# Token sums of phi on GpSimd, kv products split over two slots, and a new order for the opening of a fused attention and two-layer-MoE kernel

## The chip, the core and the metric

The kernel runs on one core of a Trainium2 chip, in one launch, on the inputs of the reference. The metric is the device time of that launch in microseconds (us), the median over runs. The core has five engines that run side by side, each with its own instruction stream executed in order: TensorE (PE in the profile, with its weight loads under PEld), VectorE (DVE), ScalarE (ACT), GpSimd (POOL) and SyncE (SP), whose queue starts nearly all DMA transfers here. An instruction that waits holds up everything behind it on its engine.

## The reference

Eight batches, eight heads, 576 tokens, head dimension 64, 32 memory slots. Attention over memories, then two dense layers:

```python
a = np.exp(phi - np.max(phi, axis=2, keepdims=True))        # over tokens
a = a / (np.sum(a, axis=2, keepdims=True) + 1e-09)
k_m = np.einsum('bhsm,bhsd->bhmd', a, k)
v_m = np.einsum('bhsm,bhsd->bhmd', a, v)
scores = scale * np.matmul(q, k_m.transpose(0, 1, 3, 2))
attn = softmax(scores)                                      # over the 32 memories
x = np.matmul(attn, v_m)                                    # -> (4608, 512)
h = x @ w_in;  g = s * np.maximum(h, 0.0)**2 + b;  x = g @ w_out       # 512 -> 2048 -> 512
# second layer: 512 -> 1024, x * softmax(x), layer norm, 1024 -> 512
```

The weights w_in and w_out are 64-bit floats of 8 MB each; they are read as pairs of 32-bit words and turned into 32-bit floats on the chip. q, k, v and phi are 32-bit floats.

## The kernel before

Work goes batch by batch; a batch's 576 tokens are two halves (j = 0, 1) of 288. For each batch the products of exp(phi) with k and v (`kv_mm`, PSUM tile `kp`) are divided by the sum of exp(phi) over the tokens (`kv_out`), giving the small memories `km`. v's memories times w_in (`vw_mm`, tile `wp`) let attention and the first layer's first product become one product (`hp` from `aT` and the folded weights); the activation is squared, and a second product with w_out gives `y`.

From batch 1 on, the code loops: `gemm1(n, j)`, then four `gemm2(n, j, d)`, and between these, `slot(n + 1, i)` with i = 0 to 7 prepares the next batch. Slot 0 held the whole of `kv_mem` (`kv_mm`, `kv_sum`, `kv_out`); slot 1 bounds the memories, slots 2 and 3 cut q and the memories into 16-bit halves, load the next batch and take the maximum of its phi, slots 4 to 6 hold scores.

Everything ahead of that, batch 0 and the preparation of batch 1, runs in an order written out by hand, the string `FIRST`. Each word is a step with its indices, and each engine's stream is the order in which the words issue instructions on it:

- `Lphi.n`, `Lkv.nu`, `Lq.ni`, `Lw.fk`, `Lo.dx` load phi, k and v (in two parts), q (four parts), a piece of w_in (8 pieces of 1 MB) and a piece of w_out (8 pieces of 1 MB), all on SP's queue (L337, L359, L368, L1128, L1142). phi has one buffer, so `Lphi.1` can start only when the readers of batch 0's phi are done; the same holds for k and v.
- `phm`, `pht`, `phd`, `pho` take phi's maximum over tokens (DVE L389, PE, DVE L400 and L404, PE); `phb` subtracts it (DVE L442), `phe` is the exponential (ACT L448).
- `km` are the 72 products per batch of phi with k and v (L478, two hardware passes each, 144 rows in the trace). `ks` is `kv_sum_all`: 72 further products of phi with a column of ones (L494), which add up the tokens in PSUM. `ko` is `kv_out`: the DVE reads the sums (L500), inverts them and scales the products.
- `qm`/`qo` transpose q (PE L547, ACT L559); `mm`, `mv`, `mk` transpose the memories; `s0` are scores (PE L830), `s1` their maximum and difference (DVE L842, L844), `s2` the exponential, `s3` sum and reciprocal, `s6` the division (DVE L863); `at`/`aA` transpose the attention.
- `Ai`, `Ci`, `PiX` decode a piece of w_in (ACT L285; DVE L289 and L290; DVE L1186); `Ao`, `Co`, `PoX` the same for w_out; `Bi`, `Bo` sums for scales (ACT L298). `vm`, `vA`, `vD` make the folded weights. `g.jp` is a quarter of the first layer for half j (PE L913), `gr`, `gs` its activation (ACT); `y.dx` half of an output column block of the second layer (PE L941); `Y` the same for half 1 (L1091).

`KEEP` gives, for some steps, a number of dummy products of a tile of ones that PE runs ahead of the step's own (L167); their result is overwritten. The only way in which the streams meet is by waits on semaphores that follow from tiles and buffers; PSUM tile `h` has three buffers, used in turn.

`kv_sum`, a single product per partition half with a precomputed sum `es` (L483), is used for batches 2 to 7, where the DVE makes `es` (`phi_sum`, inside `gemm1`).

Of the kernel before, what the change touches and what calls it, by code (L numbers as in the profile page):

```python
# [64 lines left out]
def tile_mem_attention__moe_relu2__solu_ln(  # L65
# [393 lines left out]
    def kv_mem(n):
        kv_mm(n)  # L460
        kv_sum(n)
        kv_out(n)

    def kv_cells(n):
        for c in range(CT):
# [1200 lines left out]
```

## Time and profile before

| | us |
|---|---|
| median of 3 runs (1096.86 to 1098.18) | 1097.57 |
| the profiled execution's own time | 1096.71 |
| its span, first to last instruction | 1094.9 |
| PE busy | 1058.2 (97%) |
| DVE busy | 766.3 (70%) |
| ACT busy | 523.8 (48%) |
| POOL busy | 177.5 (16%) |
| mean granted TensorE clock | 0.986 |

The span is 1.81 us under the profiled execution's time, which is 0.86 us under the median. A share of the whole span is a mean over stages: the opening (to about 170 us) is nothing like the loop behind it, so the rows below are read by stage. Idle time matters only on an engine that something later waits for.

### The profile page before, as it was taken

The page shows a single profiled execution, that of the slowest core. Times are in us where ns is not written, and L with a number is a line of the kernel's source. Part 1 is how long each engine was busy: PE and PEld are TensorE (multiplying, and loading weights), DVE is VectorE, ACT ScalarE, POOL GpSimd, SP SyncE. Part 2 cuts the span into 40 slices and gives each one's busy share as a digit, 9 for nine tenths or more (in the row PEclk, how much of TensorE's full clock was granted, in tenths as well). Part 3 has the DMA queues.
Part 4 walks back from the last instruction along what each step waited for, and adds up shares of the span by engine and source line. Part 5 has one row for each costly group of instructions (what it writes and reads, how often), then busy time and mean ns, then how long its engine had stood idle before and what let it go on. Part 6 is the DMA issues. An engine that isn't in the chain of part 4 may idle for free.

```text
span 1094.9 us, 21722 instructions
## 1 busy us (share of the span) xinstructions
PE 1058.2 (97%) x8931; PEld 699.3 (64%) x8931; DVE 766.3 (70%) x1456; ACT 523.8 (48%) x775; POOL 177.5 (16%) x165
## 2 busy tenths in 40 slices
PE   3869999999999999999999999999999999999998
PEld 2657768777777777777777777754444444444443
DVE  5468999977767768768778766467666666666662
ACT  3358875754644644654654555433323333233322
POOL 0000020221030030130120110013222221222221
PEclk9689999999999999999999999999999999999999
DMA  9885154652842932932932342124434434435324
GB/s 274 253 239 181 27 143 111 129 132 75 179 111 70 202 95 68 219 77 75 211 102 49 65 159 91 42 60 106 108 100 101 107 93 109 106 87 116 85 60 106
DMA packets 202595, 129.28 MB, mean 118 GB/s; under 512 B 137472, under 2 KB 182528, under 8 KB 202496
## 3 DMA queue, kind: packets, MB, share of 16 engines
q1 hardware_dynamic: 202352, 127.70, 46.5%
q8 instruction: 70, 1.15, 0.5%
q14 instruction: 29, 0.24, 0.1%
q10 hardware_dynamic: 112, 0.20, 0.1%
q0 software_dynamic: 32, 0.00, 0.0%
HBM read 71.83 MB, written 23.07 MB: 87 GB/s over the span
## 4 chain that ended last, share of the span: by engine, by line
PE 92%; DMA 3%; issue 2%; DVE 1%; ACT 1%; SPq 0%; ACTq 0%
PE y L1091 33%; PE y L1494 17%; PE hp L1412 17%; PE hp L1009 15%; PE hp L913 2%; PE kp L478 2%; PE wp L637 2%; PE sp L786 1%; DMA raw<-in_moe_w_in_dram 1%; DMA kv_s<-in_v_dram 1%; PE wp L595 1%; PE y L941 1%; DMA work<-kv_s 1%; PE sp L830 1%; PE tq L547 1%
## 5 line engine op out<-in xcount | busy, mean ns | idle before, releaser
L1091 PE MATMUL y<-g,w_out 128*128 128x288 f16 x2688 | 337.8, 286 | 0.5 <-issue 0.5
L1091 PEld LDWEIGHTS <-w_out 128*128 128x128 f16 x2880 | 277.6, 97 | 87.0 <-issue 13.4
L1412 PE MATMUL hp<-w_t,xs 128*128 128x512 f16 x864 | 192.0, 379 | 0.0
L1494 PE MATMUL y<-w_t,lt 128*128 128x512 f16 x864 | 191.7, 379 | 0.0
L1009 PE MATMUL hp<-aT,vwt 128*128 128x288 f16 x1344 | 166.9, 286 | 0.0
L1009 PEld LDWEIGHTS <-vwt 128*128 128x128 f16 x1344 | 131.5, 98 | 33.1
L1494 PEld LDWEIGHTS <-lt 128*128 128x128 f16 x864 | 84.6, 98 | 101.7
L1412 PEld LDWEIGHTS <-xs 128*128 128x128 f16 x864 | 84.5, 98 | 101.5
L1456 POOL TENSOR_TENSOR rstd<-ve,nhalf 128x1 f32<-128x1 f32 x36 | 52.6, 1462 | 332.4 <-DVE mv L1454 332.4
L1426 DVE TENSOR_REDUCE hmx<-hp 128x1 f32<-128x1024 f32 x36 | 44.1, 1224 | 84.1 <-PE hp L1412 84.1
L318 ACT ACTIVATE xs<-xt,xsc 128x512 f16<-128x512 f32 x36 | 25.9, 720 | 151.0 <-PE hp L1412 129.5
L1020 ACT ACTIVATE r<-hp 128x576 f32<-128x576 f32 x120 | 77.4, 645 | 26.9 <-PE hp L913 14.7
L1074 DVE TENSOR_TENSOR g<-r_s,g 128x576 f16<-128x576 f32 x112 | 85.6, 764 | 3.9
L1108 ACT ACTIVATE x<-y,bcol,cs 128x288 f32<-128x288 f32 x60 | 35.2, 586 | 106.8 <-PE y L1091 96.2
L1067 ACT ACTIVATE r_s<-r 128x576 f32<-128x576 f32 x112 | 76.6, 684 | 18.5 <-DVE g L1074 13.4
L315 DVE TENSOR_REDUCE xmx<-x 128x1 f32<-128x288 f32 x64 | 28.8, 450 | 53.0 <-ACT x L1108 52.9
L994 DVE CAST g<-r_s 128x576 f16<-128x576 f32 x112 | 52.1, 466 | 18.7 <-ACT r_s L1067 18.6
L1433 ACT ACTIVATE e<-hp,nm,xiv 128x1024 f32<-128x1024 f32 x36 | 43.3, 1203 | 45.6 <-DVE nm L1428 45.6
L1502 ACT ACTIVATE o<-y,io 128x512 f32<-128x512 f32 x36 | 24.8, 689 | 53.3 <-issue 40.8
L1470 DVE TENSOR_TENSOR nat<-so,nat 128x1024 f16<-128x1024 f32 x36 | 43.8, 1216 | 5.4 <-ACT nat L1465 5.4
L1449 DVE BATCH_NORM_STATS2 bs<-so 128x6 f32<-128x512 f32 x72 | 46.3, 685 | 1.2
L1444 DVE SCALAR_TENSOR_TENSOR so<-hp,sm,e 128x1024 f32<-128x1024 f32 x36 | 46.2, 1284 | 1.3
(240 smaller groups left out, 1191.4 us busy)
## 6 DMA issues: line engine op xcount, KB each, us to landing
kv_s<-in_k_dram SPq DMA_DIRECT2D x32, 288.0 KB, 9.1
kv_s<-in_v_dram SPq DMA_DIRECT2D x32, 288.0 KB, 9.6
x_d<-x SPq DMA_DIRECT2D x64, 144.0 KB, 1.9
xt<-x_d SPq DMA_DIRECT2D x36, 256.0 KB, 3.1
q_s<-in_q_dram SPq DMA_DIRECT2D x21, 288.0 KB, 4.6
phi_sb<-in_phi_dram SPq DMA_DIRECT2D x16, 288.0 KB, 4.3
out_dram<-o SPq DMA_DIRECT2D x23, 192.0 KB, 2.5
w_out<-in_moe_w_in_dram SPq DMA_DIRECT2D x4, 1024.0 KB, 11.0
```

Of the source, the lines that this page charges most:

```text
L994: nc.vector.tensor_copy(out=g_of(n, j, 0)[:, 2 * fp:2 * fp + 2, 0:BLK], in_=gt["r2", j, fp])
L1009: nc.tensor.matmul(out=hp[:, u, 0:BLK], lhsT=vt[:, pw, R, f * 128:(f + 1) * 128], rhs=aT[:, CJ * j:CJ * (j + 1), pa, R, :], start=(x == 0) ...
L1020: nc.scalar.activation(out=r, in_=gt.pop(("h", j, fp))[:, :, 0:BLK], func=ACTF.Relu, scale=scale)
L1067: nc.scalar.activation(out=r2, in_=r, func=ACTF.Square)
L1074: (nc.vector if eng == "D" else nc.gpsimd).tensor_tensor(out=g_of(n, j, 1)[:, fs, 0:BLK], in0=gt.pop(("r2", j, fp)), in1=g_of(n, j, 0)[:, ...
L1091: nc.tensor.matmul(out=y[:, 0:w], lhsT=w_out_t[d][:, pw, f, :], rhs=g_of(n, j, pg)[:, f, 0:w], start=(x == 0), stop=(x == len(steps) - 1),)
L1412: nc.tensor.matmul(out=hp[:, a, :], lhsT=xs[:, px, kk, :], rhs=wt[:, pw, kk, a * 512:(a + 1) * 512], start=(kk == 0 and px == 0 and pw == ...
L1426: nc.vector.tensor_reduce(out=mx, in_=hv, op=ALU.max, axis=AX)
L1444: nc.vector.scalar_tensor_tensor(out=so, in0=hv, scalar=sm[:, 0:1], in1=e, op0=ALU.mult, op1=ALU.mult)
L1449: nc.vector.bn_stats(out=bs[:, a, :], in_=so[:, a * 512:(a + 1) * 512])
L1456: nc.gpsimd.tensor_tensor(out=rstd, in0=ve, in1=nhalf, op=ALU.pow)
L1494: nc.tensor.matmul(out=y[:, 0:DM], lhsT=lt[:, pl, f, :], rhs=wt[:, pw, f, :], start=(x == 0), stop=(x == len(steps) - 1),)
```

## The change

In batches 0 and 1 the 72 products with ones are gone; five GpSimd additions (`phi_sum_pool`, step `ke`) add the nine token groups of exp(phi) down to `es`, and `ks` is now `kv_sum`, one product per partition half with ones. In later batches `kv_mm` is cut into token groups 0 to 4 in slot 0 and 5 to 8 in slot 1, and `kv_sum` and `kv_out` (with its load of the next phi) move to slot 1. The string `FIRST` and the numbers in `KEEP` are new: 35 dummies before, 109 after.

```diff
 FIRST = """
-Lw.01 Lw.00 Lphi.0 Ai.01 Ci.01 PiX.01 phm.0 Ai.00 Ci.00 Lq.02 qm.02 PiX.00 Lw.10 pht.0 phd.0 pho.0 Lkv.00 Ai.10 Lkv.01
+Lphi.0 phm.0 pht.0 phd.0 pho.0 Lw.10 Ai.10 Ci.10 PiX.10 phb.01 phb.00 Lkv.00 Lkv.01 phe.00 phe.01 ke.0 km.0 Lw.00
...
 KEEP = {
-    "pht.0": 4, "km.0": 8, "vap.0": 3, "qm.03": 1, "qm.00": 2, "qm.02": 10, "s0.00": 2, "pht.1": 4, "at.1": 1,
+    "qm.02": 4, "pht.0": 7, "pho.0": 6, "km.0": 16, "qm.00": 1, "mm.0": 8, "qm.01": 24, "qm.03": 1, "s0.01": 21,
+    "vap.0": 3, "at.1": 5, "at.0": 13,
 }
...
-    def kv_sum_all(n):
-        for out_, ph, ps, i, c, at in kv_cells(n):
-            nc.tensor.matmul(out=out_[:, 2 * D:2 * D + 1], lhsT=ph, rhs=ones[ps, :], **at)
+    def phi_sum_pool(n):
+        ph = phi_t[n]
+        t = e_p.tile([128, HG, 2, M], FP32, tag="pa", name="t", bufs=1)
+        es = e_p.tile([128, HG, M], FP32, tag="es", name="es", bufs=1)
+        for out_, x, y in (
+            (t, ph[:, :, 0:2], ph[:, :, 2:4]), (t, t, ph[:, :, 4:6]), (t, t, ph[:, :, 6:8]),
+            (es, t[:, :, 0], t[:, :, 1]), (es, es, ph[:, :, 8]),
+        ):
+            nc.gpsimd.tensor_tensor(out=out_, in0=x, in1=y, op=ALU.add)
+        es_t[n] = es
...
         if i == 0:
-            kv_mem(n)
+            kv_mm(n, range(0, 5))
...
         elif i == 1:
+            kv_mm(n, range(5, CT))
+            kv_sum(n)
+            kv_out(n)
...
-        "km": kv_mm, "ks": kv_sum_all, "ko": kv_out, "vb": vw_bound, "vs": vw_scale,
+        "km": kv_mm, "ke": phi_sum_pool, "ks": kv_sum, "ko": kv_out, "vb": vw_bound, "vs": vw_scale,
```

Three places show how the streams move. The first is SP's queue from its first transfer to the first load of batch 1's k and v; raw_g, raw and w_out are where pieces of w_in land. Before:

```order
L1128 DMA raw_g<-in_moe_w_in_dram 128x2x1024 x2
L337 DMA phi_sb<-in_phi_dram 64x4x288 x2
L368 DMA q_s<-in_q_dram 96x2x384
L1128 DMA raw<-in_moe_w_in_dram 128x2x1024
L359 DMA kv_s<-in_k_dram 64x2x576 x2
L359 DMA kv_s<-in_v_dram 64x2x576 x2
L359 DMA kv_s<-in_k_dram 64x2x576 x2
L359 DMA kv_s<-in_v_dram 64x2x576 x2
L1128 DMA raw<-in_moe_w_in_dram 128x2x1024
L368 DMA q_s<-in_q_dram 96x2x384 x2
L368 DMA wt_s<-in_q_dram 96x2x384
L337 DMA phi_sb<-in_phi_dram 64x4x288 x2
```

The same stretch of SP's queue after:

```order
L338 DMA phi_sb<-in_phi_dram 64x4x288 x2
L1135 DMA raw<-in_moe_w_in_dram 128x2x1024
L360 DMA kv_s<-in_k_dram 64x2x576 x2
L360 DMA kv_s<-in_v_dram 64x2x576 x2
L360 DMA kv_s<-in_k_dram 64x2x576 x2
L360 DMA kv_s<-in_v_dram 64x2x576 x2
L1135 DMA raw_g<-in_moe_w_in_dram 128x2x1024 x2
L369 DMA q_s<-in_q_dram 96x2x384
L338 DMA phi_sb<-in_phi_dram 64x4x288 x2
L369 DMA q_s<-in_q_dram 96x2x384 x2
L369 DMA wt_s<-in_q_dram 96x2x384
L1135 DMA raw<-in_moe_w_in_dram 128x2x1024
```

phi, then k and v, now stand ahead of all but one piece of w_in, three parts of q stand behind batch 1's phi, and k and v come behind 1.6 MB instead of 4.0 MB.

The second place is PE around batch 1's products (`km.1`, `ks.1`). Before:

```order
L830 MATMUL sp<-kmT,qt_s 96x2x32 x8
L478 MATMUL kp<-kv_s,phi_sb 32x128 x72
L494 MATMUL kp<-ones,phi_sb 32x1 x72
L913 MATMUL hp<-aT_118,vw_522 128x288 x4
L595 MATMUL wp<-w_in_t,first 32x512 x8
```

PE there after:

```order
L599 MATMUL wp<-w_in_t,first 32x512 x8
L468 MATMUL kp<-kv_s,phi_sb 32x128 x72
L480 MATMUL kp<-ones,es 128x1 x2
L917 MATMUL hp<-aT_118,vw_573 128x288 x4
L599 MATMUL wp<-w_in_t,first 32x512 x8
```

The 72 products with ones became two; the scores ahead of the products (`s0.02`, tile `sp`, L830) moved to an earlier place, and folded weights (`vm.02`) stand there instead.

The third place is the DVE's stream from phi's maximum to the division by the sums (`phm.0` to `ko.0`). Before:

```order
L389 TENSOR_REDUCE pm<-phi_sb 128x128
L289 TENSOR_SCALAR w_in_t<-w_in_t 128x2x512
L290 SCALAR_TENSOR_TENSOR w_in_t<-raw_g,w_in_t 128x2x512
L1186 SCALAR_TENSOR_TENSOR w_in_t<-raw_g,w_in_t 128x2x512
L400 TENSOR_REDUCE first<-tx 128x2
L404 TENSOR_TENSOR first<-ident,first 128x256
L442 TENSOR_TENSOR phi_sb<-phi_sb,tx 128x576
L289 TENSOR_SCALAR w_in_t<-w_in_t 128x2x512
L290 SCALAR_TENSOR_TENSOR w_in_t<-raw,w_in_t 128x2x512
L442 TENSOR_TENSOR phi_sb<-phi_sb,tx 128x576
L1186 SCALAR_TENSOR_TENSOR w_in_t<-raw,w_in_t 128x2x512
L500 TENSOR_SCALAR rs<-kp 128x2
```

The DVE there after:

```order
L390 TENSOR_REDUCE pm<-phi_sb 128x128
L401 TENSOR_REDUCE first<-tx 128x2
L405 TENSOR_TENSOR first<-ident,first 128x256
L290 TENSOR_SCALAR w_in_t<-w_in_t 128x2x512
L291 SCALAR_TENSOR_TENSOR w_in_t<-raw,w_in_t 128x2x512
L1193 SCALAR_TENSOR_TENSOR w_in_t<-raw,w_in_t 128x2x512
L443 TENSOR_TENSOR phi_sb<-phi_sb,tx 128x576
L443 TENSOR_TENSOR phi_sb<-phi_sb,tx 128x576
L290 TENSOR_SCALAR w_in_t<-w_in_t 128x2x512
L291 SCALAR_TENSOR_TENSOR w_in_t<-raw_g,w_in_t 128x2x512
L504 TENSOR_SCALAR rs<-kp 128x2
```

phi's maximum is now the DVE's first work, and one and two thirds pieces of w_in are decoded ahead of `ko.0` where before three were (the first of them ahead of the rows shown).

## Rows read from the trace of the kernel before

**Rows 1.** Who waited for whom, 0 to 80 us: total, times, longest
```profile
DVE rs L500 <- PE kp L494: 20.6, 2, 11.1
PE kp L494 <- issue: 11.8, 3, 6.3
```

**Rows 2.** Waits of SP's DMA queue, 0 to 100 us
```profile
SPq L337 <- PE kp L494: 19.7, 2, 13.0
```

**Rows 3.** PE in order of time: start, length, ..., [idle before <- releaser]
```profile
12.74 2.19 PE L547 MATMUL tq<-ident,q_s 96*64 96x96 f32 x24 [9.16 <-DMA q_s<-in_q_dram]
...
18.63 1.89 PE L167 MATMUL kp<-first 128*128 128x256 f16 x8
...
25.94 3.72 PE L478 MATMUL kp<-kv_s,phi_sb 64*32 64x128 f32 x131 [0.57 <-DMA kv_s<-in_v_dram]
...
32.94 1.27 PE L494 MATMUL kp<-ones,phi_sb 64*32 64x1 f32 x119 [3.08 <-issue]
...
43.62 2.82 PE L830 MATMUL sp<-kmT,qt_s 128*96 128x64 f32 x16
...
56.53 8.03 PE L913 MATMUL hp<-aT,vw 128*128 128x288 f32 x32
64.48 1.09 PE L595 MATMUL wp<-w_in_t,first 64*32 64x512 f32 x16
65.50 1.57 PE L830 MATMUL sp<-kmT,qt_s 128*96 128x64 f32 x16
67.00 2.25 PE L478 MATMUL kp<-kv_s,phi_sb 64*32 64x128 f32 x144
...
79.21 0.26 PE L494 MATMUL kp<-ones,phi_sb 64*32 64x1 f32 x2 [6.33 <-issue]
79.41 4.21 PE L913 MATMUL hp<-aT,vw 128*128 128x288 f32 x8
```

**Rows 4.** Stretches: length, then busy us of each engine, granted clock, DMA
```profile
core 0: us, PE busy (x) PEld busy (x) DVE busy (x) ACT busy (x) POOL busy (x), PEclk, DMA share, GB/s
0.00:56.50 56.50, 34.62 (x505) 25.54 (x505) 29.08 (x49) 20.66 (x31) 0.68 (x6) 0.82 0.91 263
34.20:53.00 18.80, 17.36 (x137) 13.32 (x137) 11.54 (x22) 8.93 (x16) 0.00 (x0) 0.50 0.93 299
56.50:69.00 12.50, 12.50 (x211) 9.61 (x212) 12.36 (x16) 11.65 (x21) 0.00 (x0) 1.00 1.05 295
69.00:79.40 10.40, 1.70 (x163) 1.52 (x143) 1.02 (x2) 1.54 (x3) 0.00 (x0) 0.73 0.62 190
79.40:170.10 90.70, 89.94 (x564) 67.22 (x563) 81.27 (x153) 66.50 (x98) 8.16 (x8) 0.97 0.45 114
```

**Rows 5.** ACT in order of time: the first and the fourth decoded piece of w_in
```profile
6.20 1.12 ACT L285 ACTIVATE w_in_t<-raw_g 128x1024 f32<-128x1024 f32 x1 [4.19 <-DMA raw_g<-in_moe_w_in_dram]
...
28.77 1.14 ACT L285 ACTIVATE w_in_t<-raw 128x1024 f32<-128x1024 f32 x1 [5.50 <-DMA raw<-in_moe_w_in_dram]
```

**Rows 6.** Groups by line and shape, 0 to 170 us: busy, mean ns | idle before
```profile
L389 DVE TENSOR_REDUCE pm<-phi_sb 128x128 f32<-128x1152 f32 x3 | 6.4, 2133 | 2.8 <-DMA phi_sb<-in_phi_dram 2.8
...
L289 DVE TENSOR_SCALAR w_in_t<-w_in_t 128x1024 int32<-128x1024 int32 x8 | 5.5, 687 | 5.7 <-ACT w_in_t L285 5.7
...
L290 DVE SCALAR_TENSOR_TENSOR w_in_t<-w_out,w_in_t 128x1024 int32<-128x1024 int32 x4 | 4.9, 1225 | 0.1
...
L1186 DVE SCALAR_TENSOR_TENSOR w_in_t<-w_out,w_in_t 128x1024 int32<-128x1024 int32 x4 | 4.8, 1218 | 0.0
```

**Rows 7.** GpSimd in order of time: two sizes of addition or product
```profile
152.94 2.61 POOL L442 TENSOR_TENSOR phi_sb<-phi_sb,px 128x1152 f32<-128x1152 f32 x1 [9.24 <-issue]
...
226.82 1.05 POOL L863 TENSOR_TENSOR e<-e,ssm 96x512 f32<-96x512 f32 x1 [11.24 <-DVE ssm L858]
```

**Rows 8.** DVE in order of time: one line beside GpSimd's work, and alone
```profile
153.23 2.87 DVE L806 TENSOR_TENSOR e<-e,smx 96x512 f32<-96x512 f32 x1
...
162.60 0.69 DVE L806 TENSOR_TENSOR e<-e,smx 96x512 f32<-96x512 f32 x1
```

**Rows 9.** PE in order of time in the loop, batch 4's sums
```profile
422.85 0.39 PE L483 MATMUL kp<-ones,es 64*128 64x1 f32 x4
```

**Rows 10.** Waits of PE, 170 us to the end: total, times, longest
```profile
PE y L1091 <- issue: 0.5, 1, 0.5
PE kp L478 <- issue: 0.4, 1, 0.4
```

More of the change, by code (lines that the diff above doesn't have):

```diff
@@ new lines @@
+Lw.01 Ai.00 Ci.00 Lq.01 ks.0 ko.0 Ai.01 PiX.00 qm.01 Lphi.1 mm.0 vb.0 Lq.02 qo.01 mv.0 phm.1 Lq.00 mk.0 Ci.01 qm.02
+qo.02 Lq.03 pht.1 Lw.11 qm.00 qm.03 Lw.20 phd.1 qo.00 qo.03 pho.1 Bi.00 PiX.01 s0.00 phb.10 Ai.11 phb.11 Lw.30 Lw.21
+s0.01 Bi.01 s1.00 s2.00 Ci.11 s3.00 PiX.11 s0.02 phe.11 Lw.31 s6.00 Bi.10 Ai.30 phe.10 Ai.20 s1.01 ke.1 Lkv.10 at.0
+aA.0 s2.01 s1.02 s3.01 Ai.21 vm.00 vad.0 vA.00 vm.01 vA.10 vA.11 s6.01 at.1 aA.1 vD.01 Ci.21 Bi.11 s2.02 vap.0 g.00
+Ci.20 g.03 Ai.31 gr.00 gs.0 s3.02 Lkv.11 g.02 PiX.20 g.01 gr.03 gs.3 Bi.20 Lo.01 Lo.11 Lsb s6.02 gr.02 gr.01 PiX.21
@@ new lines @@
+at.2 aA.2 Ci.30 Ci.31 PiX.30 vm.02 gs.2 vA.21 Lo.00 PiX.31 km.1 ks.1 vA.20 Lq.12 ko.1 gs.1 Ao.01 Bi.21 g.04 Ao.11
+Lo.10 mb.1 vm.03 mad.1 vA.30 va.0 g.05 gr.04 vb.1 vA.31 gs.4 Co.01 PoX.01 Lphi.2 vad.1 gr.05 g.06 map.1 Lq.13 Ao.00
+Co.00 PoX.00 gs.5 Lo.20 g.07 gr.06 Bi.30 ma.1 Bi.31 vap.1 Co.11 Lq.10 g.10 im y.00 va.1 gs.6 Ao.10 Bo.00 Lo.21 Lq.11
+iad PoX.11 gr.07 iap Co.10 ia PoX.10 iv vs.0 gs.7 y.01 vr Bo.01 Bo.11 cb.0 Bo.10 gr.10 g.17 yo.00 gh.0 gr.17 qa.10
+om.0 gh.7 oad.0 qa.12 gq.0 Lo.30 oap.0 oa.0 os.0 g.14 ym.00 xh.01 cc.0 qa.11 g.13 xh.00 qa.13 gq.7 xl.01 gl.0 xh.10
@@ new lines @@
+y.10 g.15 gr.14 gh.4 y.11 yd.00 gq.4 xh.11 qs.1 ms.1 Lo.31 xl.00 mm.1 Ao.20 gl.7 Ao.21 gl.4 xl.10 gr.13 gr.15 gh.3
+Co.20 PoX.20 gh.5 gq.3 Co.21 cb.1 gl.3 qh.10 Ao.30 g.12 yo.01 PoX.21 gq.5 gr.12 g.11 y.20 gl.5 gh.2 gq.2 xl.11 mv.1
+Co.30 Ao.31 mh.1 Bo.20 qh.11 Co.31 gr.11 ml.1 y.21 ym.01 gl.2 Bo.21 vm.13 yd.01 PoX.31 PoX.30 ql.10 gh.1 cb.2 g.16
+Bo.31 Bo.30 yo.02 mT.1 vs.1 qT.10 ql.11 vm.10 gq.1 vh.10 phm.2 y.30 om.1 oad.1 gl.1 qT.11 vh.13 ym.02 yd.02 gr.16
+qh.12 vl.13 ql.12 qh.13 oap.1 gh.6 gq.6 oa.1 os.1 qT.12 gl.6 ql.13 pha.2 y.31 cb.3 xh.21 yo.03 ym.03 vl.10 cc.1 vm.11
@@ L55 @@
+qT.13 vh.11 vl.11 vm.12 Y.10 xh.30 xh.20 s0.10 xh.31 sc.10 xl.30 s0.11 sc.11 xl.31 s1.11 s1.10 vh.12 vl.12 Y.00 Y.11
+s2.10 yo.11 Y.01 s3.10 phbP.2 s0.12 s6.10 Y.30 Y.31 s2.11 s3.11 s6.11 phe.2 ym.11 s4.10 s5.10 s4.11 s5.11 xl.20 yo.10
+Lkv.20 sc.12 yd.11 sT.10 s1.12 s2.12 xl.21 yd.03 s3.12 s6.12 ym.10 s4.12 sT.11 Lkv.21 yd.10 yo.13 ym.13 Y.20 Y.21
+Lq.21 yo.12 yd.13 ym.12 yd.12 Lq.20 s5.12 sT.12 Lq.22
 """
 KEEP = {
-    "pht.0": 4, "km.0": 8, "vap.0": 3, "qm.03": 1, "qm.00": 2, "qm.02": 10, "s0.00": 2, "pht.1": 4, "at.1": 1,
+    "qm.02": 4, "pht.0": 7, "pho.0": 6, "km.0": 16, "qm.00": 1, "mm.0": 8, "qm.01": 24, "qm.03": 1, "s0.01": 21,
+    "vap.0": 3, "at.1": 5, "at.0": 13,
@@ L457, in tile_mem_attention__moe_relu2__solu_ln, with kv_mm @@
     kp_t = {}
[L459 to L465, printed above, removed]
+    def kv_mm(n, cs=range(CT)):
+        if cs[0] == 0:
+            kp_t[n] = ps_h.tile([128, 2, 512], FP32, tag="h", name="kp")
+            keep(kp_t[n][:, 1, 256:512])
+        for c in cs:
             for i in range(HG):
@@ L468, in kv_cells @@
                     ps = slice(PT * a, PT * (a + 1))
-                    yield (
-                        kp_t[n][M * i:M * (i + 1), a], phi_t[n][ps, i, c, :], ps, i, c,
-                        dict(start=(c == 0), stop=(c == CT - 1), tile_position=(PT * a, M * i)),
-                    )
-    def kv_mm(n):
-        kp_t[n] = ps_h.tile([128, 2, 512], FP32, tag="h", name="kp")
-        keep(kp_t[n][:, 1, 256:512])
-        for out_, ph, ps, i, c, at in kv_cells(n):
-            nc.tensor.matmul(out=out_[:, 0:2 * D], lhsT=ph, rhs=kv_s[ps, :, i, c * D:(c + 1) * D], **at)
+                    nc.tensor.matmul(
+                        out=kp_t[n][M * i:M * (i + 1), a, 0:2 * D],
+                        lhsT=phi_t[n][ps, i, c, :],
+                        rhs=kv_s[ps, :, i, c * D:(c + 1) * D],
+                        start=(c == 0),
+                        stop=(c == CT - 1),
+                        tile_position=(PT * a, M * i),
+                    )
     def kv_sum(n):
@@ L490, in kv_sum @@
             )
-    def kv_sum_all(n):
-        for out_, ph, ps, i, c, at in kv_cells(n):
-            nc.tensor.matmul(out=out_[:, 2 * D:2 * D + 1], lhsT=ph, rhs=ones[ps, :], **at)
+    def phi_sum_pool(n):
[8 more added lines that the diff above has]
+        es_t[n] = es
     def kv_out(n):
```

19 lines of the change are left out of this document (removed).

## The prediction

> **What bounds the kernel now.** I read the stretches first, then PE in order of time, then the waits. From 170 us on nothing is to be had: PE waits there only twice, 0.5 and 0.4 us [rows 10]. Between 79.4 and 170.1 PE is busy 89.94 of 90.70 us [rows 4], so the opening's second half is PE-bound as well, with the DVE close behind (81.27 of 90.70). What is left is the time up to 79.4. There PE idles: it waits for q (9.16 us) and for k and v, and three times inside the products with ones, for "issue", 11.8 us in all and 6.33 us the longest [rows 1, 3]. "issue" means that nothing the profile knows held PE; the tiny products come so densely (119 in 1.27 us [rows 3]) that I read it as the instruction stream arriving too slowly, which is an inference. While PE stands there, the DVE stands at the division behind it (20.6 us in two waits [rows 1]), and SP's queue stands at the next phi load, whose buffer those products read (19.7 us [rows 2]). In 69.0 to 79.4 all engines are nearly idle at once [rows 4]. And PE is slow: in 34.2 to 53 the granted clock is 0.50, the 1.2 GHz level, after PE's 3.08 us stand [rows 3, 4]; the scores at 43.62 take 2.82 us where the same 16 take 1.57 at 65.50. The column says 1.00 for the first 30 us, yet 24 transposes take 2.19 us there as they do at the low level, so PE probably started low as well.
>
> **The change, part by part.**
>
> *Products with ones, batch 1.* PE leaves the kv products at about 69.1 (67.00 plus 144 rows, 2.25 with overlap) and starts the next quarter at 79.41: 10.3 us. In their place come two products in four rows, 0.39 us [rows 9]. Worth 9.9 us on PE, with no cover: everything is idle. The next quarter then also runs at the full level: 8 rows took 4.21 us, while 32 took 8.03 at 56.53, so 8 cost 2.0 [rows 3]: 2.1 us more. These 12 us follow from the removed line alone.
>
> *GpSimd's sums.* Not in the trace; nearest are 2.61 us for 1152 elements and 1.05 us for 512 [rows 7], 2.3 and 2.05 ns an element. Three additions of 256 and two of 128 are 1024 elements: about 2.2 to 2.4 us a batch, up to 5.3 if each costs as much as the 512-element row. Their cover is long: in batch 0 phi's exponential is done near 15 us while k and v land near 17 (below); in batch 1 `ke.1` stands ahead of four quarters of g, 8 us of PE. So they hold up no product. But they can hold up the DVE. Its difference L806 took 2.87 us at 153.23, when GpSimd worked on phi (152.94 to 155.55), and 0.69 at 162.60 [rows 7, 8]. That is 2.2 us lost beside one addition of 2.61. I charge 2 us for both batches; the ends are 0 and 5.
>
> The Trainium skill (SBUF — State Buffer, Who interferes with whom) says that a DVE instruction with two SBUF inputs contends with a GpSimd instruction that reads SBUF, and that the later one waits for the other's end. L806 fits that. By that rule each of the ten additions may stop one such DVE instruction for its own length, so the DVE could lose all of their 4.8 us, near the end of my bounds, and the sum below would be 3 us smaller.
>
> *The order up to the first quarter, `g.00`.* Before, it starts at 56.53. After, two chains lead there. **Loads:** the first 1 MB piece was in ACT's hands at 6.20, 5.5 us after its issue at 0.7; seven and a half MB (four pieces, phi, one part of q, k and v) had landed by 28.77 [rows 5], some 265 GB/s. At that rate, with phi first, phi lands at about 5.5, k and v behind 4.0 MB at about 17 (before: 25.9, where the products begin to stream [rows 3]), the pieces 00 and 01 at about 20 and 24, batch 1's phi at 27, the last of q at 30 to 31. q's transposes and copy add about 2.5, so scores start at 33 instead of 43.6. **The DVE:** before, it worked 29.08 us up to 56.5 [rows 4]. After, the stream up to `g.00` holds two more subtractions of phi and one more score step, less about two thirds of a decoded piece (a piece is 0.69 + 1.23 + 1.22 [rows 6]): about 30 us. It starts at 5.5 with phi's maximum (2.13 us [rows 6]), must wait some 7 us for piece 00 (from 14 to 21), and about 3 us in smaller waits for the sums and for batch 1's phi. 5.5 + 30 + 10 is 45.5; with the transposes behind it `g.00` starts at about 47, 9.5 us earlier. This swallows the 4 us that the first group of ones costs (from 29.66 to 34.21 [rows 3], less 0.39), and the low clock in front of the scores; they are not counted again.
>
> *From `g.00` to the quarter behind `km.1`.* On PE: four quarters 8.03, `vm.02` 1.09, kv products 2.25, sums 0.39 [rows 3, 9], 11.8 us, and some 1.2 us by my estimate for a transpose and a copy to wait for: 13 us, so 60 instead of 79.41. Batch 1's k and v are behind 15.5 MB, at 265 to 300 GB/s 52 to 59 us [rows 4], so just in time. Gain so far 19.4, and 2.1 for the clock: 21.5.
>
> *From there on* PE has the same work, 88.6 us at full level. The DVE's 81.27 us also move forward by nearly as much, since it stood 9.5 of its 20.6 us right there [rows 1]. The gain is kept only if the DVE does not fall further behind and w_out's pieces come 20 us earlier. 25.7 MB in all at 265 to 300 GB/s are there at 86 to 97 us; the last was needed near 107 before and at 87 after, so up to 5 us could be lost there.
>
> *Dummies.* 74 more. At the low level 8 take 1.89 us [rows 3], 0.24 each, so 17 us at most; nothing at least, where they run inside a wait. 16 stand ahead of `km.0` (a wait of 7 us), 24 ahead of q's transposes (a wait of 4 us), 21 and 13 while the DVE is the one that works. I take 0 and keep the 17 for the rivals.
>
> *The split in batches 2 to 7.* The same products, cut in two. It could save the two waits of 0.9 us in all [rows 10], or cost one more changeover in each of six batches; the nearest row is the four-row group of 0.39 us [rows 9], so 2.3 us at most. The memories are ready one slot of 6 us later, and are wanted by scores three slots on; the next phi is loaded one slot later and wanted two slots on. I take 0, from -0.9 to +2.3.
>
> *Sum.* 21.5, less 2 for the DVE beside GpSimd, less about 2.5 for handovers between engines that the walk to `g.00` leaves out (about 20 of 0.1 to 0.15 us): 17. The profiled execution would take 1096.71 - 17 = 1079.7, the median 0.86 more: 1080.6. I say **1080.5**.
>
> **The rivals.**
>
> *The tail does not follow.* The DVE's idle 9.4 us in 79.4 to 170.1 [rows 4] double because it now meets ACT and w_out's pieces, which wait for buffers that the DVE frees. For it: it is busy 90%. Against it: it moves forward with PE. Nine us less: 1089.5.
>
> *The stall stays.* If PE's stand comes from any dense run of instructions, the 144 rows of `km.1` bring it too. For it: 3.08 us stood after 131 such rows and some ones; against it: the same 144 rows in the loop are followed by at most 0.5 us [rows 3, 10], though DMA is less busy there. The removed line then gives 4 of 10 us: 1086.5 to 1088.
>
> *GpSimd on the path.* The additions at 5.3 us a batch and the DVE stopped for all of it: 3 to 5 us less, 1084 to 1086.
>
> *Slower: the clock stays low.* The new order leaves PE idle between 20 and 46 us, filled with dummies. If these do not bring the upper level, PE runs at 1.2 GHz through all eight quarters of half 0: these take 33 us instead of 16 (4.21 against 2.0 for 8 rows), scores 3.5 us more, folded weights 3.5 more, and the dummies 21 + 13 cost up to 8 us, of which perhaps half on the path. That is 28 lost where the forecast gains 17: about 1108. It decides only if the low level lasts beyond about 65 us; if it ends at 55, half of the gain is left, 1090. Against it: before, the level rose by 53 to 56 us under steady work.
>
> **How the numbers follow.** Forecast (1074 to 1085): 0.52. Tail 0.16, stall 0.13, GpSimd 0.05. Low clock 0.09, of which 0.05 slower than before. No visible gain by the tail and the clock together: 0.05. A measurement of this kernel tells 0.2%, 2.2 us, from no change. Faster 0.89, same 0.05, slower 0.06. The range from 1072 to 1093 leaves out about 0.07 below (the walk's handovers and GpSimd's charge all free, some w_out wait gone) and 0.11 above.
>
> **What would show it.** Right: no PE wait of over 1 us behind `km.1`; scores at about 33, `g.00` near 47, the quarter behind `km.1` near 60, the loop's first product near 152 instead of 170.1; GpSimd's additions 0.3 to 0.6 us each. Wrong: a new wait on PE after 60 us for w_out or the DVE (tail), "issue" of several us behind `km.1` (stall), L863 or L1186 far over their means beside GpSimd, or a granted clock of 0.50 past 55 us. If the loop from batch 1 on is more than 2 us longer than 924.8, the split cost something and my zero for it is wrong.

## The result and the profile after

The changed kernel takes **1081.45 us** (median of 4 runs, 1079.02 to 1082.55); the kernel before, timed beside it, 1097.33 us (1096.86 to 1098.18). The ratio is 0.9851, with a 95% interval of 0.9833 to 0.987: faster by about 16 us. The forecast was 1080.5 us, in a range of 1072 to 1093. The profiled execution of after took 1082.55 us (span 1080.8), the longest of its four, so marks read from it add up to 14.1 us of the 16.

PE around batch 1's products, in order of time (start, length, line, operation, tiles, count, [idle before <- releaser]); it answers to the end of [rows 3]:

```profile
51.12 8.03 PE L917 MATMUL hp<-aT,vw 128*128 128x288 f32 x32
...
61.57 2.16 PE L468 MATMUL kp<-kv_s,phi_sb 64*32 64x128 f32 x134 [0.72 <-DMA kv_s<-in_v_dram]
63.67 0.39 PE L480 MATMUL kp<-ones,es 64*128 64x1 f32 x4
63.98 2.21 PE L917 MATMUL hp<-aT,vw 128*128 128x288 f32 x8
```

Where [rows 3] has a stand of 6.33 us and then a quarter of 4.21 us at 79.41, there is now no gap, and the quarter takes 2.21 us at 63.98. The stretches between the marks (length, busy us of each engine, granted clock, DMA share, GB/s), against [rows 4]:

```profile
0.00:51.10 51.10, 34.63 (x455) 26.29 (x455) 30.86 (x52) 21.47 (x34) 6.86 (x16) 0.90 0.95 272
51.10:63.90 12.80, 12.06 (x201) 9.27 (x200) 12.59 (x17) 9.88 (x17) 0.00 (x0) 1.00 1.08 266
63.90:155.40 91.50, 88.09 (x561) 65.20 (x560) 79.23 (x152) 68.73 (x101) 7.31 (x8) 1.00 0.59 146
155.40:1080.80 925.40, 920.96 (x7516) 594.82 (x7513) 642.18 (x1237) 422.49 (x624) 167.91 (x151) 1.00 0.44 107
```

The stretch of standing still is gone. The third row is new trouble: 91.50 us for 88.09 us of PE work. All the waits of PE from 60 us to the end (total, times, longest) are these, and two of the three lie in that stretch:

```profile
PE mp L199 <- DVE first L193: 2.1, 1, 2.1
PE y L945 <- DVE first L204: 1.3, 1, 1.3
PE kp L468 <- DMA kv_s<-in_v_dram: 0.7, 1, 0.7
```

In the longest of them the DVE that PE waits for had itself waited for q, as the chain of waits shows (start, length, what):

```profile
72.48 15.59 DMA kv_s<-in_q_dram
...
88.09 0.95 DVE qmx L316
...
89.14 0.30 DVE first L193
...
89.48 0.49 PE mp L199 x2
```

A q load took 7.1 us in the kernel before (median from issue to landing, 64 to 84 us), and this one now takes 15.6. w_out's pieces are on the queues at the same time, and the DMA share is 1.07 in 60 to 90 us; I take that for the cause, which no run shows alone. In the wait of 1.3 us the DVE's step stood behind the decoding of a w_out piece, for which the DVE had waited 3.78 us for ACT, and ACT 1.63 us for the piece's load.

### The profile page after: what moved, and what is told of

It reads as the page before. It is cut to its first block, busy times and chain, and to the rows that moved or that the text cites. A ratio compares the mean times of both kernels' runs of the same rounds, so it can differ in the third digit from the quotient of the medians.

```text
span 1080.8 us, 21328 instructions
## 1 busy us (share of the span) xinstructions
PE 1055.7 (98%) x8725; PEld 695.6 (64%) x8725; DVE 764.9 (71%) x1456; ACT 522.6 (48%) x775; POOL 182.1 (17%) x175
## 4 chain that ended last, share of the span: by engine, by line
PE 92%; DMA 5%; DVE 2%; SPq 1%; issue 0%; ACT 0%; DVEq 0%; ACTq 0%
PE y L1098 33%; PE y L1501 17%; PE hp L1419 17%; PE hp L1016 15%; PE y L945 2%; PE wp L641 2%; PE kp L468 2%; DMA kv_s<-in_q_dram 1%; PE sp L790 1%; PE hp L917 1%; DMA raw<-in_moe_w_out_dram 1%; DMA kv_s<-in_v_dram 1%; DMA raw<-in_moe_w_in_dram 1%; SPq L338 1%; DMA phi_sb<-in_phi_dram 1%
## 5 line engine op out<-in xcount | busy, mean ns | idle before, releaser
L316 DVE TENSOR_REDUCE xmx<-x 128x1 f32<-128x288 f32 x64 | 28.8, 450 | 54.9 <-ACT x L1115 54.8
```

## The experiments

The marks that follow are starts on PE, in us, in one profiled execution each: the first scores, the first quarter `g.00`, the quarter behind `km.1`, and the loop's first product; then the time between the last two.

| kernel | median | scores | g.00 | quarter | loop | quarter to loop |
|---|---|---|---|---|---|---|
| before | 1097.33 | 43.62 | 56.53 | 79.41 | 169.97 | 90.6 |
| after | 1081.45 | 37.43 | 51.12 | 63.98 | 155.38 | 91.4 |
| e1, sums alone | 1079.04 | 38.16 | 51.06 | 64.04 | 153.22 | 89.2 |
| e2, no sums | 1089.45 | 41.39 | 54.79 | 73.13 | 161.73 | 88.6 |
| e3, unsplit | 1078.62 | 36.09 | 49.72 | 61.75 | 152.39 | 90.6 |
| e4, no dummies | 1080.56 | 39.47 | 55.09 | 66.73 | 153.97 | 87.2 |
| e5, sums by DVE | 1081.07 | 37.80 | 54.07 | 66.37 | 155.28 | 88.9 |
| e7, q first | 1085.65 | 44.42 | 60.06 | 71.70 | 158.94 | 87.2 |
| e8, q of batch 1 earlier | 1080.12 | 37.46 | 50.85 | 62.75 | 152.81 | 90.1 |
| e10, e3 and e8 | 1079.19 | 37.02 | 50.72 | 63.52 | 153.69 | 90.2 |
| e11, e1 with dummies | 1083.16 | 37.11 | 47.68 | 64.39 | 155.46 | 91.1 |
| e12, after again | 1081.29 | 37.80 | 51.20 | 62.84 | 154.93 | 92.1 |

### e1: the sums alone

The kernel before, with its order, its dummies and its unsplit slots; only the sums move to GpSimd.

```diff
-... phb.00 phe.00 qo.02 km.0 ...
+... phb.00 phe.00 ke.0 qo.02 km.0 ...
-... phb.10 phe.10 Ci.20
+... phb.10 phe.10 ke.1 Ci.20
-        "km": kv_mm, "ks": kv_sum_all, ...
+        "km": kv_mm, "ke": phi_sum_pool, "ks": kv_sum, ...
```

> The kernel before, in its own order and with its own dummies; only the sums of batches 0 and 1 are made by GpSimd's five additions and one product per half. Theory (the stall inside the products with ones is the larger part of the gain): the quarter behind km.1 starts near 69.5 us instead of 79.4 and runs at the full level; 10 to 12 us faster, about 1086. Rival (the new order of loads and of the DVE is the larger part; freed time is lost to the next wait): 2 to 5 us faster, 1092 to 1095.

Measured: 1079.04 us (1078.59 to 1079.91) against 1097.83, ratio 0.9837 [0.9822, 0.9851]. It is worth 18.8 us, more than either account expected, and no less than the whole change. PE in order of time:

```profile
38.16 2.82 PE L841 MATMUL sp<-kmT,qt_s 128*96 128x64 f32 x16
...
51.06 8.03 PE L924 MATMUL hp<-aT,vw 128*128 128x288 f32 x32
...
61.54 2.25 PE L478 MATMUL kp<-kv_s,phi_sb 64*32 64x128 f32 x144
63.72 0.39 PE L483 MATMUL kp<-ones,es 64*128 64x1 f32 x4
64.04 2.21 PE L924 MATMUL hp<-aT,vw 128*128 128x288 f32 x8
```

Of the two spans' difference, 16.8 us, the first group of ones gives 5.5 (`g.00` at 51.06 instead of 56.53), the second 9.9 (12.98 us from `g.00` to the quarter, 22.88 before), and what is behind the quarter 1.4, where the full clock gives 2.0. `g.00` stands where it stands in after, 51.12: the new order brought it no nearer.

### e2: the order, the dummies and the split, with the products with ones

```diff
-        "km": kv_mm, "ke": phi_sum_pool, "ks": kv_sum, ...
+        "km": kv_mm, "ke": lambda n: None, "ks": kv_sum_all, ...
```

> The changed kernel with its new order, dummies and split, but with the 72 products with ones per batch instead of GpSimd's additions. Theory (stall): PE stands again for several us behind km.0 and km.1 and the gain left is 3 to 6 us, 1091 to 1094. Rival (order): 10 us or more remain, 1084 to 1087.

Measured: 1089.45 us (1088.94 to 1090.03) against 1097.83, ratio 0.9932 [0.9916, 0.9949]: 8.4 us, between the two expectations. PE in order of time:

```profile
66.17 0.74 PE L505 MATMUL kp<-ones,phi_sb 64*32 64x1 f32 x54
72.27 0.94 PE L505 MATMUL kp<-ones,phi_sb 64*32 64x1 f32 x80 [5.36 <-issue]
73.13 3.08 PE L927 MATMUL hp<-aT,vw 128*128 128x288 f32 x6
```

The stand behind `km.1` is there again, 5.36 us for 8.70 before; the other stand of this kernel inside the ones is 1.36 us. So the order is worth something where the ones are kept: the two stands add up to 6.7 us instead of 11.8. Once the ones are gone, it is worth nothing that can be told (e3 against e1, next). The two parts overlap: 18.8 and 8.4 are worth 16 to 19 together.

### e3 and e12: what the split costs

e3 is after with the slots unsplit; e12 is after again, word for word, timed beside e10 (e3 with one load moved, below).

```diff
         if i == 0:
-            kv_mm(n, range(0, 5))
+            kv_mm(n)
+            kv_sum(n)
+            kv_out(n)
...
         elif i == 1:
-            kv_mm(n, range(5, CT))
-            kv_sum(n)
-            kv_out(n)
```

> The changed kernel with all of the kv products, the sums and the division back in slot 0 for batches 2 to 7. Theory (the split is worth nothing): within 2 us of the changed kernel, and the loop from batch 1's first product to the end 0 to 1 us shorter. Rival (a slot's worth of instructions at once costs PE waits): PE waits of 0.4 us and more behind these products come back and the loop is 1 to 3 us longer.

> The changed kernel again, word for word, on the same chip as e10 and e11. Expected 1080 to 1082 us; against e10 it gives the price of the split and of the load's place in one call: 2 to 3 us if the split costs 0.31 us a batch over six batches and the load's place 0.5 to 1, under 1 us if the differences between calls made them.

Measured: e3 1078.62 us (1078.29 to 1078.85), ratio 0.9832 [0.9817, 0.9846]; e12 1081.29 us (1079.37 to 1083.35), ratio 0.986 [0.9845, 0.9875]. By these medians the split costs 2.7 us, but the two intervals still touch; against e10 (1079.19), which was timed beside it, e12 is 2.1 us slower, at the low end of the larger of its two expectations. The loops tell how much of that is the split's own. PE in after, batch 4's products:

```profile
405.60 1.37 PE L468 MATMUL kp<-kv_s,phi_sb 64*32 64x128 f32 x80
...
412.93 1.16 PE L468 MATMUL kp<-kv_s,phi_sb 64*32 64x128 f32 x64
```

The same batch in e3:

```profile
401.63 2.15 PE L468 MATMUL kp<-kv_s,phi_sb 64*32 64x128 f32 x130
404.08 0.45 PE L468 MATMUL kp<-kv_s,phi_sb 64*32 64x128 f32 x14 [0.30 <-issue]
```

Two pieces take 1.37 + 1.16 = 2.53 us where one run of 144 takes 2.25: 0.3 us more a batch, in six batches 1.7 to 1.9. Against it the split avoids the short waits for "issue" (0.3 us here, 0.7 in e10, 0.9 in e1, [rows 10] in before; none in after and e12). From the loop's first product to the end it is 925.4 us in after and e12, 924.1 in e3, 924.7 in e10 and 924.9 in e1: the split costs 0.5 to 1.3 us. The rest of e3's lead, 1 to 3 us, is there when the loop begins, where the two programs still have the same instructions; why e3's opening ran faster in its runs is left open.

### e4: no dummies

```diff
-KEEP = {
-    "qm.02": 4, "pht.0": 7, ..., "at.0": 13,
-}
+KEEP = {}
```

> The changed kernel without any of its 109 dummy products. Theory (dummies lie inside waits and hold the clock): the granted clock falls to 0.50 somewhere between 20 and 60 us, scores and the first quarters slow down, 3 to 8 us slower than the changed kernel. Rival (dummies stand on PE's path): 1 to 4 us faster.

Measured: 1080.56 us (1079.64 to 1081.9), ratio 0.9851 [0.9836, 0.9865]: the same as after, so neither expectation came about. But the opening runs slowly. First the stretch of e4 from 34 to 56 us (columns as in after's stretches, the granted clock ahead of the DMA share), then two rows of its PE in order of time:

```profile
34.00:56.00 22.00, 20.18 (x156) 15.58 (x154) 17.79 (x30) 14.92 (x25) 3.63 (x5) 1.00 1.04 333
```

```profile
28.18 2.19 PE L548 MATMUL tq<-ident,q_s 96*64 96x96 f32 x24 [1.50 <-DMA q_s<-in_q_dram]
...
39.47 7.94 PE L831 MATMUL sp<-kmT,qt_s 128*96 128x64 f32 x48
```

24 transposes take 2.19 us, as at the 1.2 GHz level, where after has 1.21 at the 2.4 GHz level; the 48 rows of scores take 7.94 us, where after has 1.65 for 16 and 2.85 for 32. The clock column nevertheless reads 1.00 in that stretch: this trace's first clock record stands at 54.9 us, and the column shows 1.00 where there is none. `g.00` comes 4 us later than in after, and the loop begins 1.4 us earlier. The dummies do what they are for, and it is worth nothing at the end.

### e5: the DVE makes the sums

```diff
-        "km": kv_mm, "ke": phi_sum_pool, "ks": kv_sum, ...
+        "km": kv_mm, "ke": phi_sum, "ks": kv_sum, ...
```

> The changed kernel with the sums of batches 0 and 1 made by the DVE (one reduction of 2.1 us each) in the place of GpSimd's additions. Theory A (the DVE is what is late between 35 and 50 us, so its work there is on the path up to g.00, but the opening's end is set later, by w_out's and q's loads): g.00 some 2 to 4 us later, the loop's start at most 1 us later. Theory B (as the prediction has it: what g.00 loses, the end loses): 3 to 4 us slower than the changed kernel.

Measured: 1081.07 us (1080.15 to 1082.47), ratio 0.9844 [0.9826, 0.9861]: no difference, although `g.00` and the quarter come 3.0 and 2.4 us later. What is gained comes from the products that are no longer there; that GpSimd adds is not what matters.

### e6: products with ones in the loop

After, with the 72 products with ones in place of the two, in slot 1 of batches 2 to 7.

```diff
             kv_mm(n, range(5, CT))
-            kv_sum(n)
+            kv_sum_all(n)
```

> The changed kernel, but in batches 2 to 7 the 72 products with ones stand in slot 1 behind the second part of the kv products, in place of the one product per half; the opening is unchanged. Theory (a dense run of small instructions outruns the instruction stream, and the more so the busier DMA is): each batch's products with ones take 1.5 us busy and PE stands 1 to 3 us, 12 to 25 us slower in all. Rival (the stand needs the opening's full DMA queue): 1.5 to 2 us a batch with no wait, 7 to 10 us slower.

A single run: 1095.64 us, 14.2 over after's median, as the theory has it (12 to 25) and not the rival (7 to 10). In the loop's first batch PE reads

```profile
173.53 1.21 PE L505 MATMUL kp<-ones,phi_sb 64*32 64x1 f32 x117
177.44 0.40 PE L505 MATMUL kp<-ones,phi_sb 64*32 64x1 f32 x27 [2.70 <-issue]
```

and its waits from 170 us to the end are

```profile
PE kp L505 <- issue: 4.9, 2, 2.7
PE y L1108 <- issue: 2.1, 2, 1.8
```

7.0 us of standing in six batches: the stands come with these products in the loop as well, but 1.2 us a batch, while the opening of before had 3.08 and 8.70. The other 7 us or so are the products' own work.

### e7 and e8: two loads moved

In e7 three parts of q go ahead of batch 1's phi; in e8 the first part of batch 1's q goes ahead of a w_out piece; e10 is e3 with e8's load.

```diff
-(e7) ... qm.01 Lphi.1 mm.0 vb.0 Lq.02 qo.01 mv.0 phm.1 Lq.00 mk.0 Ci.01 qm.02 qo.02 Lq.03 pht.1 ...
+(e7) ... qm.01 mm.0 vb.0 Lq.02 qo.01 mv.0 Lq.00 Lq.03 Lphi.1 phm.1 mk.0 Ci.01 qm.02 qo.02 pht.1 ...
-(e8) ... gs.5 Lo.20 g.07 gr.06 Bi.30 ma.1 Bi.31 vap.1 Co.11 Lq.10 g.10 ...
+(e8) ... gs.5 Lq.10 Lo.20 g.07 gr.06 Bi.30 ma.1 Bi.31 vap.1 Co.11 g.10 ...
```

> The changed kernel with the last three parts of batch 0's q loaded ahead of batch 1's phi, whose load waits 10.1 us in SP's queue for the kv products; phi's maximum moved behind accordingly. Both theories: q's last part lands 2 to 4 us earlier and scores start at 34 to 36 us instead of 37.4. Theory A (the end is set by loads up to 90 us): the total moves by less than 2 us. Theory B (what the scores gain, the end gains): 2 to 4 us faster.

> The changed kernel with one load, a part of batch 1's q (288 KB, 15.6 us from issue to landing in the changed kernel), put ahead of a 1 MB piece of w_out. Theory A (the DVE's wait for that q, 2.24 us, and PE's 2.13 us behind it are the tail that does not follow): both waits go and the kernel is 1.5 to 3 us faster. Rival (the queue is full to 90 us, and w_out's piece is as late as q was): within 1 us of the changed kernel.

> The changed kernel with its slots unsplit (as in e3) and Lq.10 ahead of Lo.20 (as in e8). If the two add, 1077 to 1078 us, some 1 us under e3's 1078.62; if the end takes up what the opening gains, 1078.3 to 1079, as e3.

Measured: e7 1085.65 us (1083.44 to 1089.54), ratio 0.9892 [0.9866, 0.9918]; e8 1080.12 (1079.26 to 1081.12), 0.9839 [0.9821, 0.9856]; e10 1079.19 (1078.16 to 1080.15), 0.9841 [0.9826, 0.9855], beside e12's 1081.29. e7 misses by both accounts: phi arrived at 36.7 and the DVE stood, which held back q's steps behind it (the DVE's waits up to 60 us, the first row):

```profile
DVE pm L390 <- DMA phi_sb<-in_phi_dram: 11.5, 2, 7.1
```

So q and phi cannot both be early. e8 begins the loop 2.6 us earlier than the profiled execution of after, with PE waits of 1.9 us there in place of 3.4, but its median is only 1.3 us lower and its interval overlaps; e10 is not under e3 and lies just above both of its expectations. The load's place is worth about 1 us at most, and that isn't shown.

### e9: wider products with ones

The kernel before, with as many products in the same places, each 384 columns wide in place of one; only the first column is used.

```diff
-            nc.tensor.matmul(out=out_[:, 2 * D:2 * D + 1], lhsT=ph, rhs=ones[ps, :], **at)
+            nc.tensor.matmul(out=out_[:, 2 * D:512], lhsT=ph, rhs=ones[ps, :].to_broadcast([PT, 384]), **at)
```

> The kernel before, with each product against ones as wide as the state's columns allow (384 columns in place of 128), so that as many instructions stand in the same places and are used up more slowly. Its sums are the same. Supply theory (PE stands because tiny products are used up faster than the sequencer delivers them): 72 x 2 products take about 3 x 2.18 = 6.5 us of PE at the full clock, and the waits with no releaser behind km.1 shrink from 8.7 us to at most 2, so 7 to 9 us from the last kv product to the quarter behind it, against 10.3 before. Rival (the stand has nothing to do with how dense the products are): 6.5 us of work and 8.7 us of standing, about 15 us.

A single run: 1097.95 us. PE behind `km.1`:

```profile
69.84 0.84 PE L494 MATMUL kp<-ones,phi_sb 64*32 64x384 f32 x9
74.55 7.57 PE L494 MATMUL kp<-ones,phi_sb 64*32 64x384 f32 x130 [3.87 <-issue]
82.06 2.21 PE L913 MATMUL hp<-aT,vw 128*128 128x288 f32 x8
```

Neither expectation holds: the stand is 3.87 us, not under 2 and not 8.7, and the whole takes 12.2 us. The stands of both groups shrink from 11.8 to 5.8 us. Slower use shortens the stands, as the supply theory says, but by half only; the kernel's time stays where it was, since work has taken the place of standing.

### What arrives in a stand

The profile's page lists a queue of the kind "instruction" among the DMA queues. In after it moved

```profile
q8 instruction: 68, 1.11, 0.5%
```

that is 68 packets of 16 KB. PE ran 8725 products and as many weight loads there, 17450 instructions, 257 to a packet: this queue carries PE's stream, as I read it. Before has 70 packets for 8931 products. One packet begins in or just ahead of each of the stands at and behind the products with ones (the times are of the half microsecond in which it begins). In before they are found in 30.0 to 30.5, 34.0 to 34.5, 69.0 to 69.5 and 76.5 to 77.0, and PE goes on after a stand at 32.94, 36.95, 71.65 and 79.21: 2.2 to 2.5 us behind the end of that half microsecond each time (the delays that follow are counted so too). e2: 26.0 to 26.5 and 69.5 to 70.0, on at 28.83 and 72.27 (2.3 us). e9: 30.0 to 30.5 and 71.5 to 72.0, on at 32.58 and 74.55 (2.1 and 2.6). e1, behind its first sums: 30.0 to 30.5, on at 32.95 (2.5). e6 in the loop: 174.0 to 174.5 and 259.5 to 260.0, on at 177.44 and 262.61 (2.9 and 2.6). e3's gap of 0.30 us: 401.5 to 402.0, on at 404.08 (2.1). With e11's, below, these are thirteen stands in seven kernels, all ended 2.1 to 2.9 us behind a packet. Not every wait called "issue" is one: the 1.5 us in after, inside the first kv products at some 20 us, has no packet within 15 to 24.

The stands also keep a count. In PE's rows the first of them comes behind the 220th product in before, e1, e2 and e9 alike, whether it stands at a product with ones or, as in e1, at a transpose of q; and from one stand to the next in before it is 128 products, with their loads 256 instructions (119 + 2 + 7 rows from 32.94 to 36.95, and 128 from 71.65 to 79.21):

```profile
36.95 1.60 PE L547 MATMUL tq<-ident,q_s 96*64 96x96 f32 x17 [1.44 <-issue]
...
71.65 1.24 PE L494 MATMUL kp<-ones,phi_sb 64*32 64x1 f32 x128 [2.37 <-issue]
```

So where PE can stand hangs on how many instructions have run and not on what the next one is; whether it does hangs on the pace. In after the 220th product comes among the transposes of q from 29.59 on, 3 us behind the packet of 26.0 to 26.5, and there is no stand. At these places I read "issue" as the wait for the next 16 KB of PE's instructions: it rests on the packets' times and on this count, and no run changed the packets alone. The 72 products of a batch with k and v and the 72 with ones are 288 rows in the trace with 288 weight loads, 576 instructions, over two packets in some 3.5 us; the sums from `es` leave 296, little over one.

The Trainium skill (Runtime: NRT & Kernel Launch, Instruction fetch mechanics) says that each engine's instructions are streamed in blocks of 16 KiB or 256 instructions, fetched ahead while the ones before run, and that crossing a block is mostly hidden. The size agrees with the 257 worked out above; that crossing is hidden does not hold in the stands above, where by this reading it cost up to 6.3 us a time.

Why the packet before the longest stand came only at 76.5, when PE had stood since 72.9 and the DMA share was 0.29 in 69 to 75, stays open.

### e11: dummies in e1

```diff
-    "pht.0": 4, "km.0": 8, ..., "qm.00": 2, "qm.02": 10, ...
+    "pht.0": 4, "km.0": 8, ..., "qm.00": 24, "qm.02": 10, ...
```

> e1 (the kernel before with GpSimd's sums alone) with 24 dummy products at qm.00 in place of 2, so that PE is busy ahead of the scores. Theory A (the end takes up 2 to 3 us): PE faster in the opening, the quarter behind km.1 2 to 3 us earlier than e1's 64.04, the total within 1 us of e1's 1079.04. Theory B (the end follows the quarter): 1076 to 1077.5 us.

Measured: 1083.16 us (1081.38 to 1086.42), ratio 0.9887 [0.9871, 0.9904]: slower than e1, by neither theory's account. PE in order of time:

```profile
47.68 8.03 PE L924 MATMUL hp<-aT,vw 128*128 128x288 f32 x32
...
58.16 2.25 PE L478 MATMUL kp<-kv_s,phi_sb 64*32 64x128 f32 x144
60.33 0.39 PE L483 MATMUL kp<-ones,es 64*128 64x1 f32 x4
64.39 3.87 PE L924 MATMUL hp<-aT,vw 128*128 128x288 f32 x8 [3.67 <-ACT wt_s L285]
```

The clock came up, `g.00` is 3.4 us earlier than in e1, and then PE stands 3.67 us behind `km.1`, though the products with ones are gone; the quarter runs at the low level, 3.87 us for 2.21, and the lead is lost. The releaser named cannot be the cause: in e1 the same instruction of ACT starts at 65.85, after the quarter. But a packet landed in the stand, 2.4 us before its end (the queues from 61.5 to 62.0: packets, MB, share of 16 engines):

```profile
q8 instruction: 1, 0.02, 14.1%
```

So the stands do not need products with ones, though this one's cause is read from the packet alone. In e1 the packet came at 65.0 and left one gap of 0.27 us at 67.78 (2.3 us behind it); in after it came at 67.5, while PE had longer products to run, and no gap is seen. What the change did, then, was to thin out the stream at one place; where the next stand falls goes, by the count above, with the number of instructions ahead of it, and no run set that number on purpose.

## Why the prediction was right, and where it was not

**Products with ones, batch 1: right.** The 9.9 us on PE are the 9.9 that e1 shows between `g.00` and the quarter. The full clock behind it, forecast at 2.1 us, is 2.0 (4.21 less 2.21). The inference that PE's instructions arrive too slowly is borne out by the packets and by the count of instructions between stands. The rival "the stall stays" is out for this kernel, with no wait for "issue" behind `km.1`; that any dense run could bring a stand has a case after all in e11.

**The first group of ones: mis-sized, and in the wrong term.** It was put at 4 us and said to be swallowed by the new order. Alone it is worth 5.5 us at `g.00` (e1). In before its stand of 3.08 us and one of 1.44 behind it lay on the path to the scores. e1 still has one of 1.44 there, at 32.95; gone are the 3.08, the 1.2 us by which the products outlast the sums that replace them, and about 1 us that 24 transposes lost to the low clock (2.50 us in before, 1.45 in e1).

**The order up to `g.00`: the step that failed.** 9.5 us were expected there, to 47; it came at 51.12, 5.4 earlier, and e1 gets these without the order. The walk's chain was the DVE's, with 30 us of work and 15.5 of waits (5.5 to its start, 7 for piece 00, 3 more). The work was right, 30.86 us; the waits came to 19.5. The first piece of w_in was in ACT's hands at 11.62, and the DVE stood 3.33 us for it, a wait that the walk does not have; for piece 00 it stood 7.84. The kv products streamed at 21.62, not 17, and phi's next load waited in SP's queue for them, with q's parts behind it. The DVE's waits for w_in up to 51 us and SP's for the kv products in after, and the DVE's stand at phi's maximum (total, times, longest; then a row in order of time):

```profile
DVE w_in_t L290 <- ACT w_in_t L286: 11.2, 2, 7.8
```

```profile
SPq L338 <- PE kp L468: 10.1, 1, 10.1
```

```profile
32.14 2.13 DVE L390 TENSOR_REDUCE pm<-phi_sb 128x128 f32<-128x1152 f32 x1 [2.60 <-DMA phi_sb<-in_phi_dram]
```

The walk took 265 GB/s as constant from the first load on, where the first 20 us moved 215, and let phi and q arrive as if nothing in the queue waited for a buffer. So the scores began at 37.43, not 33. From 32.14 on the DVE had no wait up to `g.00`: its lateness was complete by then, and that q's own delay held `g.00` is not shown.

**From `g.00` to the quarter: right.** 13 us forecast, 12.86 measured; the quarter at 63.98 instead of 60 carries the 4 us from above and nothing else.

**From there on: 88.6 forecast, 91.4 measured.** The kernel gives 2.8 us back, at the place that was named ("w_out's pieces come 20 us earlier", up to 5 us): PE stood 2.1 us through a part of q behind them and 1.3 us through a piece of w_out itself. The table shows the pattern behind it: with the quarter near 62 to 64 us the stretch takes 89.2 to 92.1 us, with the quarter at 66 to 73 it takes 87.2 to 88.9 (before's 90.6 holds 2.0 of the low clock, e11's 91.1 holds 1.7). Of a shift of the quarter only a part reaches the end. That is the rival "the tail does not follow" at a third of its price.

**GpSimd's sums: charged 2, cost nothing seen.** GpSimd in after, batch 1 (batch 0 reads the same at 18.68 to 22.07):

```profile
45.85 0.73 POOL L497 TENSOR_TENSOR t<-phi_sb 128x256 f32<-128x256 f32 x1 [23.78 <-ACT phi_sb L449]
46.66 1.53 POOL L497 TENSOR_TENSOR t<-t,phi_sb 128x256 f32<-128x256 f32 x2
48.27 0.46 POOL L497 TENSOR_TENSOR es<-t 128x128 f32<-128x128 f32 x1
48.81 0.45 POOL L497 TENSOR_TENSOR es<-es,phi_sb 128x128 f32<-128x128 f32 x1
```

The additions take 3.2 us a batch, over the 2.2 to 2.4 taken and inside the bound of 5.3. Beside these the DVE does its score steps at 0.67 to 0.69 us, as elsewhere; beside batch 0's it waits for w_in. In e1 the same additions lie beside the decoding of w_in:

```profile
57.88 2.72 POOL L504 TENSOR_TENSOR t<-t,phi_sb 128x256 f32<-128x256 f32 x2
60.68 0.79 POOL L504 TENSOR_TENSOR es<-t 128x128 f32<-128x128 f32 x1
61.55 1.32 POOL L504 TENSOR_TENSOR es<-es,phi_sb 128x128 f32<-128x128 f32 x1
```

```profile
57.13 1.23 DVE L289 TENSOR_SCALAR w_in_t<-w_in_t 128x1024 int32<-128x1024 int32 x1
58.39 1.63 DVE L290 SCALAR_TENSOR_TENSOR w_in_t<-w_out,w_in_t 128x1024 int32<-128x1024 int32 x1
```

There 5.7 us of additions instead of 3.2, and the DVE loses 0.4 us at L290 (1.23 alone, [rows 6]) and 0.5 at L289 (0.69 alone), some 2 us in the five instructions from 57.1 to 64, as much as the charge. It was off the path all the same: PE reached `ks.1` at 63.72 without a wait. The rule of the Trainium skill that the prediction weighed (SBUF — State Buffer, Who interferes with whom) fits e1's L290, with two inputs in SBUF; L289 has one and is not covered by it. In after the subtractions L848 have one input in PSUM, and nothing was lost there. The charge of the DVE for all of the additions did not come about in either.

**Dummies: right at 0** (e4). **The split: 0 taken, 0.5 to 1.3 measured**, inside -0.9 to 2.3. The loop is 0.5 us longer than before's, below the 2 us that were to prove the zero wrong.

**The slow clock did not come:** 1.00 from 51.1 on, and the quarter at 2.21.

**The sum.** 17 us forecast from the profile; 14.1 in the profiled execution, which is the longest, and 15.9 by the medians beside each other. The total was right because errors cancel, which is luck: the walk to `g.00` promised 4 us too much, the tail 2.8; the 4.5 us charged for GpSimd and for handovers were not spent in their places. No row or run shows the 2.5 us for handovers. The attribution was off by more than the total. The text makes the removed line worth 12 us and the order the rest; alone, the removed line with its sums is worth 18.8, and order, dummies and split bring nothing on top of it that the runs can tell, or cost 2 us.

## What to carry to other kernels

Before reordering an opening, take out the one run of instructions during which everything stands, alone, and time that: here it was the whole gain, and the order that came with it hid this. The tiny products cost more by their number here than by their work (e9: 384 times the columns, and the kernel's time within 1.2 us), and an idle PE with no releaser is worth holding against the packets of the queue that carries its instructions. An earlier mark in the opening is not an earlier end: read who will then meet on the DMA queues behind it.
